# The order table of a fused linear-attention and MLP kernel is replaced by another one

## The chip, the cores and the metric

The kernel runs on one core of a Trainium2 chip. The metric is the device time of one execution in microseconds (us). The engines are PE (TensorE), DVE (VectorE), ACT (ScalarE), POOL (GpSimd) and SP (SyncE), which here only issues DMAs. Each works through its own list of instructions in order; semaphores make one engine wait for another.

## The reference

Two stages: a linear attention with a decaying state, and a two-layer MLP on its output.

```python
for t in range(S):                                   # B, H, S, D = 4, 8, 768, 48
    kt, vt, rt = (k[:, :, t], v[:, :, t], r[:, :, t])
    cur = np.einsum('bhd,bhe->bhde', u[None] * kt, vt)
    y[:, :, t] = np.einsum('bhd,bhde->bhe', rt, state + cur)
    state = w[None, :, :, None] * state + np.einsum('bhd,bhe->bhde', kt, vt)
x = y.transpose(0, 2, 1, 3).reshape(3072, 384)
h = x @ w_in                                         # 384 x 2048
sp = np.maximum(h, 0.0) + np.log1p(np.exp(-np.abs(h)))
out = (h * erf(sp)) @ w_out                          # 2048 x 384
```

## The kernel before

The sequence is cut into chunks of 128 steps, four batches each: 24 chunks, numbered 0 to 23, four of which fill one block of 512 tokens for the MLP. There are six blocks (0 to 5). The MLP takes 16 pieces of 128 of its 2048 hidden columns per block, so 96 MLP steps, numbered 0 to 95. Block 0 does its first eight pieces (steps 0 to 7), then block 1 its first eight (8 to 15), then the two finish (16 to 31), and the other blocks follow whole. MLP step 8 is therefore the first that needs block 1, that is, chunks 4 to 7.

All work is written as short words in a table, `ORDER`. A loop reads the table and issues the instructions of each word; the order of the words is the order of the instructions on every engine, since each engine keeps the order in which it was given work. Numbers in a word are those of the chunk or the MLP step. A `+` at a word's end puts it on POOL, a `*` on ACT, nothing on DVE (or on the one engine that can do it). The words, with the lines of the profile:

- `L4a`, `L4b`: load the two halves of chunk 4 (L66, L69), 512 and 608 KB. `U0` loads `ub` (L76). `F12` loads a piece of a weight as 64-bit words (L102; first digit 0 for `w_in`, 1 for `w_out`), 768 KB, into one of two `raw` buffers. `C12a` to `C12f` turn that piece into two fp32r parts (L118 to L130; `a` and `e` are on ACT, the rest on DVE, `f` may be on POOL) in one `wt` buffer, so pieces follow each other.
- `K`, `R`, `N` (L187, L191, L195) scale a chunk; `Qa`, `Qb`, `Qc` (L212, L215, L219) make the diagonal's sums `q`; `M70`, `M71` (L230 on ACT, L232 elsewhere) write them into `am`; `A7` (L249, PE) makes the chunk's scores; `P70`, `P71` (L255, DVE) merge the scores into `am`; `Y7` (L272, PE) is the chunk's output; `X7a`, `X7b` (L312 ACT, L315 DVE) write it into the block's `x`. `D7` (L291, PE) is the state's update, `S7a` to `S7d` (L303 to L309) add it to `sbd`.
- An MLP step n: `f` (L338, PE, nine matmuls `x`,`wih`/`wil` to `h`), `a b z c d e g` (the activation, ACT except `z` and `g`, L345 to L370), `h` (L376, ACT) and `l` (L381, DVE or POOL) split it into `gh` and `gl`, and `p` (L397, PE, nine matmuls into `acc`).
- `W8` issues eight matmuls on zeros (L87, `dummy`), which only keep PE at work.

Chunks live in three buffers of one pool (chunk 3 in another): a load waits until an earlier chunk's last reader is done. `h` has three PSUM buffers; `A`, `D` and, from chunk 4 on, `Y` share two more. SP's list is in order too: a load behind a waiting one waits with it.

Of the kernel before, what the change touches and what calls it, by code (L numbers as in the profile page):

```python
# [615 lines left out]
S0b S0a L3a C00a P01 Q1b+ Q2c W7 A2 L3b N2 M21* C00b Y0 N1 M20* C00c D2 L4a K3+ S2b X0a S2a X0b L4b P20 R3 W7 D1 C00d
Q3a C00e F01 S1b K4+ Q1c P21 M11* C00f+ S1a W11 Y2 M10* P11 Q3b+ X2a P10 C10a Q4a W4 Y1 C10b Q3c N3+ A3 X1a L5a X2b
M30* X1b R4+ D3 L5b S3a M31* P30 C10c L6a P31 R5+ L6b S3b W10 A4 K5 Q4b Y3 C10d X3a R6 F11 C10e X3b N4+ W4 f0 Q4c Q6a+
M41* Q5a+ M40* P41 f1 Q5b+ a0 P40 b0 N5+ Q5c z0 A5 a1 M50* C10f K6 b1 P50 C01a z1 W7 Y4 M51* C01b C01c c0 c1 C01d X4a
d1 X4b F02 C01e Q6b P51 e1 C01f+ d0 g1 W11 A6 e0 Q6c f2 M60* g0 N6 C11a P60 h0 f3 C11b h1 l0 a2 C11c M61* C11d Y5 b2  # L620
l1 F03 C11e z2 a3 p0 C11f X5a b3 X5b C02a P61 p1 c2 C02b d2 C02c e2 z3 D6 g2 c3 Y6 C02d h2 d3 l2 F12 C02e S6a p2 S6b
e3 C02f X6a g3 S6d+ C03a X6b f4 h3 C03b C03c C03d D5 a4 f5 S5a b4 F13 S5b C03e S5d z4 S5c c4 C03f D4 a5 f6 d4 S4a L7a
l3 C12a S4c S6c L7b e4 C12b b5 g4 p3 a6 C12c L8a h4 b6 R7 C12d f7 Q7a C12e F05 l4 C12f p4 R8 L9a C13a z5 Q7b+ z6 c5
# [1 line left out]
g6 L10b S7d+ Q8c h6 Q9a+ S7a M80* C13c f9 a8 C13d M81* R9 F14 C13e l5 A8 b8 l6+ z7 p5 P81 a9 C13f+ c7 P80 b9 z8 d7 A9
c8 Q10a+ e7 p6 d8 Q9b+ g7 C14a Q10b+ Q9c e8 f10 h7 M90+ g8 M91* Q10c l7+ P90 h8 P91 f11 a10 l8+ z9 b10 c9 N10 C14b p7
d9 N9 a11 C14c O70a b11 O70b C14d O71a Y9 e9 O71b S7c N8 C14e g9 D8 C14f h9 f12 O72a l9 C05a O72b z10 C05b c10 p8 z11
a12 C05c d10 c11 C05d e10 p9 d11 g10 F04 C05e S4d R10 h10 C05f f13 e11 F15 b12 g11 l10 h11 z12 f14 l11+ a13 C04a K10
c12 C04b b13 p10 C04c a14 d12 C04d b14 e12 p11 z13 F06 C04e g12 c13 C04f h12 f15 d13 l12 C15a z14 e13 C15b c14 p12 g13
a15 C15c d14 h13 C15d e14 f16 b15 l13+ F16 g14 C15e h14 z15 C15f+ p13 a16 c15 b16 l14 C06a f17 z16 d15 C06b c16 C06c  # L630
e15 d16 p14 C06d a17 e16 g15 F07 C06e g16 f18 h15 C06f h16 l15 b17 C16a l16+ z17 p15 a18 O150a C16b c17 O150b C16c
O151a f19 d17 O151b C16d b18 e17 F17 z18 C16e g17 O152a C16f f20 h17 O152b c18 l17 C07a p16 d18 C07b a19 C07c e18 b19
g18 p17 a20 z19 h18 C07d b20 c19 l18+ f21 C07e d19 C07f e19 z20 C17a p18 g19 a21 C17b h19 C17c b21 f22 c20 l19 d20
C17d e20 z21 C17e p19 g20 c21 C17f a22 d21 f23 X9a e21 X9b h20 g21 b22 l20 h21 Y8 z22 a23 l21+ c22 b23 p20 S8a L11a
M100+ S8b d22 z23 X8a M101+ e22 L11b X8b c23 g22 p21 d23 S8c S8d h22 R11 e23 K11 A10 O230a g23 l22+ O232a h23 f24 P101
Q11a+ P100 l23 f25 Q11b+ a24 b24 Q11c N11+ z24 A11 M110 a25 c24 M111 p22 b25 P111 d24 z25 e24 P110 c25 p23 g24 d25
O230b h24 e25 O230c l24+ Y11 g25 O232b h25 O232c l25+ D11 X11a f26 O231a S11a S11b S11c+ X11b S11d D9 a26 Y10 S9a L12a
b26 S9c O231b z26 O231c f27 X10a S9b L12b c26 S9d X10b d26 R12 e26 f28 a27 g26 b27 K12 z27 Q12a+ f29 c27 a28 Q12b d27
Q12c N12+ b28 A12 e27 M120+ a29 g27 M121* p24 P120 b29 P121 p25 h26 l26 z28 Y12 c28 h27 d28 l27+ D12 X12a e28 f30 X12b
g28 S12b S12a S12d+ z29 f31 a30 S12c c29 b30 d29 D10 a31 p26 S10b L13a e29 S10d b31 g29 S10a L13b S10c p27 h28 L14a  # L640
l28 R13+ z30 L14b p28 c30 K13+ h29 d30 L15a e30 l29 A13 R14 L15b z31 K14+ p29 g30 c31 h30 Q13a d31 Q13b f32 l30 O311a
e31 N13 O312a Q13c R15+ g31 M130* p30 M131+ a32 P130 h31 K15 b32 f33 P131 l31+ z32 Q15a c32 p31 Q15b a33 d32 Q15c N15+
b33 O311b e32 z33 Y13 O311c O312b c33 g32 O312c d33 D13 Q14a X13a f34 e33 S13a L16a S13b S13c+ h32 X13b S13d+ g33
O310a l32 h33 L16b f35 Q14b a34 l33+ Q14c b34 M140* z34 K16+ O310b f36 a35 O310c M150* R16+ p32 c34 Q16a a36 Q16b d34
N14 b35 M141 e34 A15 z35 N16+ b36 g34 c35 p33 M151+ P150 h34 d35 P151 e35 l34 f37 g35 z36 h35 Q16c c36 l35+ f38 a37
d36 b37 e36 z37 p34 a38 g36 c37 b38 d37 f39 h36 e37 l36+ g37 p35 a39 z38 b39 c38 d38 f40 h37 e38 l37 g38 Y15 a40 z39
b40 c39 D15 X15a d39 f41 S15b S15d e39 X15b g39 S15a f42 S15c a41 b41 A14 p36 P140 P141 p37 h38 l38 z40 Y14 a42 c40
b42 d40 D14 M161 X14a p38 L17a S14b e40 X14b S14d+ h39 S14a g40 S14c+ L18a l39 f43 h40 z41 L18b l40+ c41 d41 L17b z42
A16 a43 R18+ e41 p39 P161 c42 K18+ b43 g41 d42 Q18a+ e42 p40 h41 g42 Q17a+ l41 f44 h42 Q17b+ z43 c43 l42 d43 Q18b f45
a44 Q17c N18+ e43 b44 g43 z44 p41 a45 M171 c44 N17 b45 K17 d44 p42 R17 h43 M160 e44 M170 g44 f46 l43 h44 z45 l44+ Q18c  # L650
c45 f47 P160 a46 d45 b46 e45 z46 Y16 a47 g45 c46 b47 d46 p43 M180 X16a M181+ e46 X16b g46 p44 h45 l45 z47 p45 c47 h46
d47 l46+ e47 A17 g47 h47 p46 P171 l47+ P170 Y17 D17 X17a f48 X17b S17b S17a S17d+ S17c+ f49 a48 b48 z48 f50 c48 a49
d48 b49 e48 A18 z49 a50 g48 c49 p47 P181 h48 b50 l48 d49 P180 O470a f51 z50 O472a O470b e49 O472b c50 g49 d50 Y18 a51
h49 e50 l49+ D16 X18a g50 f52 L19a b51 S16b O471a S16d S16a L20a z51 S16c+ X18b p48 c51 L20b a52 d51 R19 b52 K19+
O471b p49 e51 h50 L19b g51 K20+ A19 h51 R20+ f53 Q20a l50 l51+ z52 p50 c52 Q20b+ a53 d52 Q19a+ Q20c b53 p51 e52 z53
N20+ g52 c53 Q19b+ h52 f54 d53 l52+ Q19c e53 g53 M191+ f55 h53 M201+ a54 P191 b54 l53+ z54 f56 a55 N19+ c54 b55 M190+
d54 z55 p52 a56 P190 e54 c55 g54 b56 p53 d55 h54 e55 l54+ M200* g55 f57 z56 h55 c56 l55 d56 f58 a57 e56 b57 g56 p54
z57 a58 b58 c57 d57 p55 h56 e57 l56 z58 f59 g57 c58 h57 d58 l57+ e58 A20 a59 g58 p56 b59 P200 P201 z59 p57 h58 c59
l58+ d59 e59 p58 g59 h59 l59+ f60 p59 a60 b60 z60 f61 c60 d60 e60 g60 f62 a61 h60 b61 l60 z61 p60 a62 c61 b62 d61 z62
f63 e61 c62 g61 d62 h61 D19 e62 l61+ Y19 a63 g62 b63 h62 p61 S19a X19a S19c S19b l62+ X19b z63 S19d p62 c63 d63 e63  # L660
g63 f64 h63 l63 p63 a64 b64 O630a z64 O631a O630b f65 c64 O631b d64 e64 f66 g64 a65 O632a b65 O632b h64 z65 f67 a66
l64+ c65 b66 d65 z66 p64 a67 c66 e65 d66 g65 D18 b67 Y20 S18a L21a h65 S18c e66 S18b l65+ g66 L21b f68 X20a S18d+ z67
h66 X20b l66+ c67 L22a d67 p65 a68 K21+ L22b e67 b68 R21 L23a f69 z68 Q21a+ g67 c68 L23b K22+ h67 d68 f70 Q22a+ a69
e68 l67+ b69 g68 A21 a70 Q22b+ z69 b70 p66 R23+ Q22c c69 d69 Q21b e69 N21 p67 h68 R22 M220* Q23a Q21c Q23b+ g69 f71
M210+ h69 N23+ P210 f72 a71 N22 l68 b71 l69 z70 p68 M211 a72 c70 M221+ P211 b72 z71 p69 d70 Q23c c71 K23 e70 d71 g70
Y21 e71 h70 g71 l70 h71 f73 X21a M231+ z72 M230* X21b l71 c72 f74 a73 d72 b73 e72 z73 A22 a74 g72 c73 p70 P221 b74 d73
P220 e73 g73 p71 h72 l72+ f75 z74 h73 c74 l73+ d74 f76 e74 a75 g74 b75 z75 f77 a76 c75 b76 d75 A23 a77 e75 p72 b77 g75
P231 P230 f78 h74 l74+ z76 Y23 c76 a78 d76 p73 b78 X23a e76 X23b Z0 g76 p74 h75 l75+ f79 z77 h76 c77 l76+ d77 p75 e77
z78 a79 g77 c78 b79 d78 Y22 h77 e78 l77 g78 p76 X22a X22b z79 c79 f80 h78 d79 l78 e79 g79 p77 a80 b80 z80 p78 c80 h79
d80 l79+ e80 f81 g80 h80 l80 p79 a81 b81 O790a z81 O791a O790b f82 c81 O791b d81 e81 f83 g81 a82 O792a b82 O792b h81  # L670
z82 f84 a83 l81+ c82 b83 d82 z83 p80 a84 e82 b84 g82 c83 p81 h82 d83 l82 e83 z84 p82 g83 c84 h83 d84 l83+ e84 f85 g84
h84 l84 f86 a85 b85 z85 p83 c85 a86 d85 b86 p84 e85 z86 g85 c86 h85 d86 f87 l85+ e86 g86 h86 p85 a87 l86 b87 z87 p86
c87 d87 e87 f88 g87 h87 l87+ f89 a88 b88 z88 f90 c88 a89 d88 b89 p87 e88 z89 a90 g88 c89 h88 f91 b90 l88 d89 z90 e89
c90 g89 p88 a91 d90 b91 h89 f92 e90 l89+ g90 h90 z91 p89 a92 l90+ c91 b92 d91 z92 f93 e91 c92 g91 d92 h91 f94 a93 l91+
# [67 lines left out]
```

## Time and profile before

| | us |
|---|---|
| median of three runs (528.63 to 529.61) | 529.5 |
| the profiled execution | 532.55 |
| its span, first to last instruction | 530.7 |
| PE busy | 512.3 |
| ACT busy | 397.1 |
| DVE busy | 348.6 |
| POOL busy | 170.5 |

The span is the part of the profiled execution that the trace covers; 1.85 us lie around it. Busy times are sums over the whole span; the stages differ, so the views by stage matter more. "Idle before" a group is the time its engine stood still ahead of it, with the engine that ended the wait.

### The profile page before, as it was taken

The page shows a single profiled execution, that of the slowest core. Times are in us where ns is not written, and L with a number is a line of the kernel's source. Part 1 is how long each engine was busy: PE and PEld are TensorE (multiplying, and loading weights), DVE is VectorE, ACT ScalarE, POOL GpSimd, SP SyncE. Part 2 cuts the span into 40 slices and gives each one's busy share as a digit, 9 for nine tenths or more (in the row PEclk, how much of TensorE's full clock was granted, in tenths as well). Part 3 has the DMA queues.
Part 4 walks back from the last instruction along what each step waited for, and adds up shares of the span by engine and source line. Part 5 has one row for each costly group of instructions (what it writes and reads, how often), then busy time and mean ns, then how long its engine had stood idle before and what let it go on. Part 6 is the DMA issues. An engine that isn't in the chain of part 4 may idle for free.

```text
span 530.7 us, 10435 instructions
## 1 busy us (share of the span) xinstructions
PE 512.3 (97%) x4151; PEld 395.7 (75%) x4159; DVE 348.6 (66%) x609; ACT 397.1 (75%) x757; POOL 170.5 (32%) x152
## 2 busy tenths in 40 slices
...
PEclk9999996999999999999999999999999999999999
...
GB/s 304 315 238 67 94 234 230 91 172 76 159 72 127 101 156 211 23 147 1 42 134 1 1 137 98 2 0 2 41 278 3 1 2 1 41 20 1 1 1 65
DMA packets 13863, 48.91 MB, mean 92 GB/s; under 512 B 1648, under 2 KB 1776, under 8 KB 13808
## 3 DMA queue, kind: packets, MB, share of 16 engines
...
q8 instruction: 35, 0.57, 0.5%
...
## 4 chain that ended last, share of the span: by engine, by line
PE 82%; DVE 9%; ACT 6%; DMA 1%; issue 1%; SPq 0%; DVEq 0%; ACTq 0%
PE acc L397 36%; PE h L338 35%; PE y L272 6%; PE A L249 3%; ACT am L230 2%; DMA att<-in_att_dram 1%; PE ds L291 1%; DVE am L255 1%; DVE att L191 1%; DVE s L354 1%; DVE wt L122 1%; DVE wt L125 1%; ACT s L345 1%; ACT s L362 1%; DVE q L219 1%
## 5 line engine op out<-in xcount | busy, mean ns | idle before, releaser
L338 PE MATMUL h<-x,wih 128*128 128x512 f32 x576 | 184.7, 402 | 2.3 <-DVE x L315 1.1
L381 POOL TENSOR_TENSOR gl<-s,gh 128x512 fp32r<-128x512 f32 x48 | 64.5, 1344 | 225.4 <-ACT gh L376 207.9
L338 PEld LDWEIGHTS h<-x,wih 128*128 128x128 f32 x576 | 107.9, 190 | 30.4 <-DVE s L370 2.0
L397 PE MATMUL acc<-gh,woh 128*128 128x512 f32 x288 | 116.3, 404 | 0.0
L338 PE MATMUL h<-x,wil 128*128 128x512 f32 x288 | 114.6, 398 | 0.0
L397 PE MATMUL acc<-gh,wol 128*128 128x512 f32 x288 | 113.8, 395 | 0.3 <-DVE wol L130 0.3
L397 PE MATMUL acc<-gl,woh 128*128 128x512 f32 x288 | 113.8, 395 | 0.3 <-DVE gl L381 0.2
L370 DVE SCALAR_TENSOR_TENSOR s<-s,h 128x512 f32<-128x512 f32 x96 | 65.6, 684 | 61.6 <-ACT s L366 61.2
L354 DVE SCALAR_TENSOR_TENSOR s<-s,h 128x512 f32<-128x512 f32 x96 | 65.6, 684 | 49.9 <-ACT s L349 39.7
L376 ACT CAST gh<-s 128x512 fp32r<-128x512 f32 x96 | 58.9, 616 | 36.0 <-PE acc L397 17.5
L358 ACT ACTIVATE s<-s 128x512 f32<-128x512 f32 x96 | 60.1, 627 | 29.1 <-DVE s L354 28.8
L345 ACT ACTIVATE s<-h 128x512 f32<-128x512 f32 x96 | 56.7, 591 | 26.9 <-PE h L338 23.0
L397 PEld LDWEIGHTS acc<-gh,woh 128*128 128x128 f32 x288 | 54.2, 188 | 15.9 <-issue 2.6
L338 PEld LDWEIGHTS h<-x,wil 128*128 128x128 f32 x288 | 54.7, 190 | 13.2 <-DVE wil L130 0.4
L397 PEld LDWEIGHTS acc<-gh,wol 128*128 128x128 f32 x288 | 54.2, 188 | 13.3 <-DVE wol L130 0.7
L397 PEld LDWEIGHTS acc<-gl,woh 128*128 128x128 f32 x288 | 54.2, 188 | 12.9 <-DVE gl L381 1.0
L366 ACT ACTIVATE s<-s 128x512 f32<-128x512 f32 x96 | 60.3, 628 | 1.1
L362 ACT ACTIVATE s<-s 128x512 f32<-128x512 f32 x96 | 60.1, 626 | 0.9
L349 ACT ACTIVATE s<-s 128x512 f32<-128x512 f32 x96 | 60.1, 626 | 0.8
L255 DVE COPY_PREDICATED am<-mask,A 64x256 f32<-64x256 uint32 x96 | 39.5, 443 | 13.2 <-ACT am L230 5.2
L381 DVE TENSOR_TENSOR gl<-s,gh 128x512 fp32r<-128x512 f32 x48 | 36.1, 753 | 17.3 <-ACT gh L376 17.1
L230 ACT ACTIVATE am<-ident,q 128x128 f32<-128x128 f32 x100 | 31.3, 390 | 8.8 <-DVE q L219 8.7
...
## 6 DMA issues: line engine op xcount, KB each, us to landing
...
att<-in_att_dram SPq DMA_DIRECT2D x24, 512.0 KB, 4.0
raw<-in_win_dram SPq DMA_DIRECT2D x8, 768.0 KB, 4.4
raw<-in_wout_dram SPq DMA_DIRECT2D x8, 768.0 KB, 4.2
...
```

Of the source, the lines that this page charges most:

```text
L255: nc.vector.copy_predicated(out=am[r, :, c], data=ap[r, :, c], mask=m[r, hh:hh + 1, c].to_broadcast([r.stop - r.start, NPAIR, H]))
L338: nc.tensor.matmul(out=h, lhsT=w[:, f, q, :], rhs=x[:, xi, q, :], start=k == 0, stop=k == 8)
L345: nc.scalar.activation(out=s1, in_=e["h"], func=AF.Tanh, bias=FB0, scale=FA0)
L349: nc.scalar.activation(out=s1, in_=s1, func=AF.Tanh, bias=FB1, scale=FA1)
L354: nc.vector.scalar_tensor_tensor(out=e["s"], in0=e["s1"], scalar=FG, in1=e["h"], op0=ALU.mult, op1=ALU.add)
L358: nc.scalar.activation(out=s, in_=s, func=AF.Tanh, bias=FB2, scale=FA2)
L362: nc.scalar.activation(out=s, in_=s, func=AF.Square, bias=FB3, scale=FA3)
L366: nc.scalar.activation(out=s, in_=s, func=AF.Square, bias=FB4, scale=FA4)
L370: nc.vector.scalar_tensor_tensor(out=s, in0=s, scalar=FC, in1=ff[n]["h"], op0=ALU.subtract, op1=ALU.mult, reverse0=True)
L376: nc.scalar.copy(out=e["gh"], in_=e["s"])
L381: eng.tensor_tensor(out=e["gl"], in0=e["s"], in1=e["gh"].bitcast(F32), op=ALU.subtract)
L397: nc.tensor.matmul(out=acc[e], lhsT=w[:, f, es], rhs=g, start=first and i == 0, stop=last and i == 2)
```

## The change

Only the table changes: 1717 words become 1719. The computation's words are the same in both; what differs is their order, which engine some of them are put on (`K3`, for instance, moves from POOL to DVE), and the dummy words: 73 matmuls in ten words become 70 in twelve. The start of the table and the rows that lead to `f8`, cut from the diff:

```diff
-L0a L1a U0 L0b R0 L2a T0 K0 Q0a+ L2b A0 K1 L1b R1 K2 W4 A1 R2 F00 Q0b Q2a+ Q0c M00* N0 F10 Q2b+ W8 D0 M01* P00 Q1a+
+U0 L0a L0b L1a R0 T0 L2a K0 Q0a W1 A0 Q0b L3a Q0c N0+ M01* L2b K1+ W4 D0 S0b M00* P01 R1+ S0a F00 P00 W7 A1 R3 K3 Y0
...
-L8b K7+ Q7c a7 S4b d5 N7+ M71* L9b A7 M70+ e5 P71 b7 K8+ P70 c6 D7 g5 d6 Y7 Q8a e6 K9 h5 C13b X7a L10a S7b Q8b+ X7b f8
+L7b c6 z7 S4c+ d6 p5 C13b c7 C13c L8a e6 d7 K7 L8b R7 e7 Q7a A7 g7 Q7b+ L9a g6 Q7c h6 L9b C13d M70* N7 M71* F05 l6+
+P70 C13e P71 K9+ h7 Y7 l7+ R9+ D7 X7a L10a X7b f8 C13f L10b Q9a C05a S7a S7b S7c+ p6 a8 S7d C05b b8 C05c p7 C05d O70a
```

The first place is on DVE, around the sum `q7` of chunk 7 (L219), the last chunk of block 1. Before:

```order
L191 TENSOR_TENSOR att8_1040<-att8_1040,wr_110 112x512
L354 SCALAR_TENSOR_TENSOR s2_5_1078<-s1_5_1001,h5_970 128x512
L354 SCALAR_TENSOR_TENSOR s2_6_1081<-s1_6_1037,h6_1003 128x512
L219 TENSOR_REDUCE q7_1086<-att7_1015 128x8
L305 TENSOR_TENSOR sbd_143<-sbd_143,ds4_992 48x4x48
L255 COPY_PREDICATED am7_1_1093<-mask_94,A7_1_1100 64x4x64
```

and after:

```order
L187 TENSOR_TENSOR att7_1076<-att7_1076,wk_111 112x512
L191 TENSOR_TENSOR att7_1076<-att7_1076,wr_110 112x512
L212 TENSOR_TENSOR att7_1076<-att7_1076,ub_85 128x384
L370 SCALAR_TENSOR_TENSOR s2_7_1084<-s2_7_1084,h7_1030 128x512
L370 SCALAR_TENSOR_TENSOR s2_6_1061<-s2_6_1061,h6_993 128x512
L219 TENSOR_REDUCE q7_1132<-att7_1076 128x8
L125 SCALAR_TENSOR_TENSOR wt13_1074<-raw13_955,wt13_1074 128x768
```

The scaling of chunk 7 by `wk` is now on DVE and stands just ahead of the sum, and so do the steps `g7` and `g6` of the MLP; ahead of `q7` DVE has 157 instructions, where it had 152.

The second place is on PE, the end of the work ahead of chunk 7's scores. Before:

```order
L397 MATMUL acc0_1_841<-gl_4_1061,woh_91 128x512
L397 MATMUL acc0_1_841<-gh_4_1042,wol_92 128x512
L397 MATMUL acc0_2_842<-gh_4_1042,woh_91 128x512
L397 MATMUL acc0_2_842<-gl_4_1061,woh_91 128x512
L397 MATMUL acc0_2_842<-gh_4_1042,wol_92 128x512
L249 MATMUL A7_0_1099<-att7_1015 64x128
```

and after:

```order
L397 MATMUL acc0_1_790<-gl_5_1063,woh_91 128x512
L397 MATMUL acc0_1_790<-gh_5_1047,wol_92 128x512
L397 MATMUL acc0_2_791<-gh_5_1047,woh_91 128x512
L397 MATMUL acc0_2_791<-gl_5_1063,woh_91 128x512
L397 MATMUL acc0_2_791<-gh_5_1047,wol_92 128x512
L249 MATMUL A7_0_1109<-att7_1076 64x128
```

The word `p5` has moved ahead of `A7`; otherwise PE has the same useful words ahead of `f8` in both tables. Behind `f8` the runs of attention words (`A`, `Y`, `D`) that interrupt the MLP's matmuls number 37, where they were 34.

The third place is on POOL, the work that leads to the step `Qb` of chunk 7 (L215). Before:

```order
L130 TENSOR_TENSOR wil_90<-wt01_656,wih_89 128x768
L309 TENSOR_TENSOR sbd_143<-sbd_143,wp_109 48x4x48
L215 TENSOR_TENSOR att7_1015<-att7_1015 128x384
L187 TENSOR_TENSOR att7_1015<-att7_1015,wk_111 112x512
L195 TENSOR_TENSOR att7_1015<-att7_1015,wkn_142 128x384
L232 TENSOR_TENSOR am7_0_1117<-ident_93,q7_1086 128x512
```

and after:

```order
L130 TENSOR_TENSOR wil_90<-wt01_604,wih_89 128x768
L195 TENSOR_TENSOR att6_591<-att6_591,wkn_142 128x384
L130 TENSOR_TENSOR wol_92<-wt11_807,woh_91 128x768
L309 TENSOR_TENSOR sbd_143<-sbd_143,wp_109 48x4x48
L381 TENSOR_TENSOR gl_3_989<-s2_3_887,gh_3_973 128x512
L309 TENSOR_TENSOR sbd_143<-sbd_143,wp_109 48x4x48 x2
L381 TENSOR_TENSOR gl_5_1063<-s2_5_1007,gh_5_1047 128x512
L309 TENSOR_TENSOR sbd_143<-sbd_143,wp_109 48x4x48 x2
L215 TENSOR_TENSOR att7_1076<-att7_1076 128x384
```

Between the weight piece `wt01` and chunk 7 POOL had one instruction and now has nine; the scaling of chunk 7 and the writing of `am7` (both `M70` and `M71` are now on ACT) have left it. On SP the loads of chunk 7 now stand behind the load of the weight piece `raw14`, which stood behind chunks 7 to 10 before.

More of the change, by code (lines that the diff above doesn't have):

```diff
@@ L614 @@
 ORDER = """
-L0a L1a U0 L0b R0 L2a T0 K0 Q0a+ L2b A0 K1 L1b R1 K2 W4 A1 R2 F00 Q0b Q2a+ Q0c M00* N0 F10 Q2b+ W8 D0 M01* P00 Q1a+
[L616 to L623, printed above, removed]
-L8b K7+ Q7c a7 S4b d5 N7+ M71* L9b A7 M70+ e5 P71 b7 K8+ P70 c6 D7 g5 d6 Y7 Q8a e6 K9 h5 C13b X7a L10a S7b Q8b+ X7b f8
@@ L625 @@
[L625 to L674, printed above, removed]
@@ L675 @@
-e92 b93 g92 p90 z93 a94 b94 c93 d93 p91 h92 e93 l92+ g93 f95 h93 z94 l93 c94 d94 p92 a95 e94 b95 g94 z95 p93x h94 p93y
-c95 l94 d95 p93z e95 p94x g95 p94y h95 p94z l95 p95x p95y O950a p95z O950b O951a O951b O952a O952b
+U0 L0a L0b L1a R0 T0 L2a K0 Q0a W1 A0 Q0b L3a Q0c N0+ M01* L2b K1+ W4 D0 S0b M00* P01 R1+ S0a F00 P00 W7 A1 R3 K3 Y0
+F10 R2 K2 Q2a W2 A2 X0a L1b Q2b C00a Q2c N2+ X0b M21* C00b W4 D2 L3b C00c M20* S2b C00d Q1a C00e F01 Q1b C00f+ Q1c P20
+M11* L4a P21 M10* Q3a+ P11 W20 Y2 L4b Q3b+ S2a C10a P10 X2a C10b W2 Y1 R4 X2b K4+ A3 X1a Q3c X1b M30* N3 N1 W2 D3 M31*
@@ new lines @@
+Q4a D1 S3a Q4b+ L5a S1a P30 P31 L5b C10c W7 A4 C10d Y3 R5 C10e F02 S1b K5+ X3a Q4c X3b M41* W4 f0 S3b L6a Q5a C10f
+M40* L6b P41 Q5b+ C01a f1 P40 N5+ a0 Q5c b0 M50+ M51* z0 A5 R6+ a1 P50 c0 C01b b1 W3 Y4 C01c d0 e0 z1 X4a C01d c1 d1
+X4b F11 K6 C01e g0 e1 C01f+ P51 h0 g1 W14 A6 l0 C02a f2 N4 h1 C02b C02c l1 f3 a2 C02d b2 z2 C02e F03 Q6a p0 c2 C02f a3
+d2 Q6b C11a Q6c N6+ p1 M61* C11b C11c M60* f4 C11d b3 P60 C11e F12 P61 e2 C11f+ Y5 a4 g2 b4 z3 h2 f5 X5a l2 C03a X5b
+c3 C03b d3 C03c Y6 a5 e3 C03d b5 D6 g3 F13 X6a p2 C03e S6b S6a S6d+ z4 h3 S6c c4 C03f d4 D5 X6b l3+ C12a f6 S5a S5b e4
@@ new lines @@
+S5c+ z5 S5d+ g4 c5 p3 C12b a6 d5 C12c h4 C12d e5 f7 b6 g5 F14 C12e l4 h5 C12f D4 a7 z6 l5+ p4 C13a L7a S4b S4a b7 S4d+
+L7b c6 z7 S4c+ d6 p5 C13b c7 C13c L8a e6 d7 K7 L8b R7 e7 Q7a A7 g7 Q7b+ L9a g6 Q7c h6 L9b C13d M70* N7 M71* F05 l6+
+P70 C13e P71 K9+ h7 Y7 l7+ R9+ D7 X7a L10a X7b f8 C13f L10b Q9a C05a S7a S7b S7c+ p6 a8 S7d C05b b8 C05c p7 C05d O70a
+z8 C05e O70b K10 f9 c8 Q8a O72a Q8b d8 K8 O72b e8 Q10a f10 R8 a9 O71a g8 Q10b+ b9 O71b Q8c h8 N8+ Q10c A8 z9 a10 l8+
+b10 f11 c9 M81+ z10 d9 e9 C05f+ P81 c10 p8 a11 g9 d10 M80 h9 b11 N10 f12 P80 e10 l9+ C14a g10 z11 h10 A9 a12 C14b c11
@@ new lines @@
+C14c p9 b12 d11 C14d e11 Q9b F04 C14e g11 f13 N9+ Q9c h11 l10+ M91* F06 f14 C14f+ z12 M90* P91 c12 P90 a13 p10 l11
+C04a R10 b13 C04b a14 z13 p11 d12 C04c c13 b14 C04d d13 e12 D9 F15 Y9 C04e g12 e13 C04f h12 f15 g13 C06a l12+ S9a S9b
+h13 S9d+ z14 f16 l13 a15 C06b c14 b15 C06c d14 D8 C06d a16 p12 e14 z15 F07 b16 g14 C06e S9c c15 C06f f17 h14 d15 l14
+C15a z16 p13 e15 C15b a17 g15 c16 C15c b17 f18 d16 C15d h15 e16 F16 l15 C15e z17 p14 a18 C15f c17 b18 g16 C07a p15 d17
+C07b O150a C07c O151a O150b e17 f19 C07d O151b h16 g17 C07e F17 l16 h17 f20 C07f a19 O152a l17 C16a O152b z18 p16 b19
@@ new lines @@
+C16b c18 C16c a20 d18 z19 p17 b20 C16d e18 C16e g18 c19 C16f f21 h18 d19 l18 C17a z20 p18 e19 C17b c20 g19 a21 C17c
+d20 f22 b21 C17d e20 C17e g20 h19 C17f f23 h20 l19 a22 X9a z21 b22 p19 X9b a23 l20 c21 b23 z22 d21 p20 c22 e21 d22 g21
+e22 Y8 h21 g22 l21 h22 z23 f24 l22+ M100* L11a S8b S8a c23 S8c+ L12a S8d+ X8a p21 d23 X8b a24 M101 e23 K11 b24 g23 p22
+O231a z24 R12+ h23 L11b c24 K12+ d24 A10 O232a e24 L12b g24 f25 l23 h24 R11 P100 l24+ f26 a25 P101 b25 Q11a+ z25 Q11b+
+f27 c25 a26 Q12a+ Q11c d25 b26 N11 M110* A11 z26 Q12b+ p23 Q12c N12+ c26 P110 a27 d26 O231b e25 e26 Y10 O231c g25 b27
```

39 lines of the change are left out of this document (added).

## The prediction

> **What bounds the kernel now.** I read the page first, then the windows, and then the timelines of the stretch that stands out.
>
> ```profile
> span 530.7 us, 10435 instructions
> PE 512.3 (97%) x4151; PEld 395.7 (75%) x4159; DVE 348.6 (66%) x609; ACT 397.1 (75%) x757; POOL 170.5 (32%) x152
> PEclk9999996999999999999999999999999999999999
> ```
>
> PE is busy 97% of the span, and its clock is full in every fortieth but the seventh (80 to 93 us).
>
> ```profile
> 60.00:80.00 20.00, 19.69 (x172) 14.95 (x171) 19.72 (x34) 14.83 (x25) 3.20 (x2) 1.00 0.56 188
> 80.00:100.00 20.00, 16.77 (x175) 12.40 (x177) 15.31 (x28) 13.67 (x32) 13.45 (x12) 0.74 0.56 207
> 100.00:120.00 20.00, 20.00 (x176) 16.12 (x174) 17.93 (x30) 18.75 (x35) 5.33 (x5) 1.00 0.36 119
> 480.00:520.00 40.00, 40.00 (x174) 32.36 (x173) 16.08 (x24) 33.31 (x60) 7.79 (x6) 1.00 0.00 1
> ```
>
> The columns are PE, weight loads, DVE, ACT, POOL, granted clock. Up to 80 us DVE has no air (19.72 of 20); from 100 us on PE is full, to the end. So the order can matter in one place only: how soon PE gets enough work to stay full. That is decided at MLP step 8, which waits for chunk 7.
>
> ```profile
> 80.81 0.39 PE L397 MATMUL acc<-gh,wol 128*128 128x512 f32 x1
> 81.87 0.43 PE L249 MATMUL A<-att 48*64 48x128 f32 x2 [0.67 <-POOL att L187]
> 82.87 1.05 PE L249 MATMUL A<-att 48*64 48x128 f32 x30 [0.57 <-DVE sbd L305]
> 85.31 0.88 PE L291 MATMUL ds<-att 128*48 128x48 f32 x16 [1.38 <-DVE am L255]
> 86.12 1.51 PE L272 MATMUL y<-att,sbd 112*32 112x128 f32 x24
> 87.40 1.94 PE L272 MATMUL y<-am,att 128*32 128x128 f32 x32
> 89.94 1.39 PE L338 MATMUL h<-x,wih 128*128 128x512 f32 x2 [0.60 <-ACT x L312]
> 86.00:88.00 2.00, 2.00 (x41) 1.78 (x41) 1.97 (x5) 1.47 (x3) 1.17 (x1) 0.50 0.00 0
> ```
>
> PE ends `p4` at 81.2, gets `A7` late, waits for `am`, runs `D7` and `Y7` at half clock (0.50), and starts `f8` at 89.94. From there to the end of the span are 530.7 - 89.94 = 440.8 us.
>
> **The change part by part.** *PE's own list.* Ahead of `f8` the new list holds one word more, `p5`; the rest of its useful words is the same. So what follows `f8` is shorter by one `p`:
>
> ```profile
> 59.91 2.09 PE acc L397 x9
> 64.16 2.29 PE acc L397 x9
> ```
>
> 2.1 us less. The second row is such a word behind an attention word: 0.2 us more. Behind `f8` there are 37 runs of attention words instead of 34, so 3 x 0.2 = 0.6 us more. The change ends where the old kernel does if `f8` starts 2.1 - 0.6 = 1.5 us later, at 91.4.
>
> *DVE up to `q7`.* The sum `q7` stands behind 157 instructions of DVE instead of 152: five more `Qa`/`Qb`, three `g`, a `z`, two steps of a weight piece, against fewer `R`, `N`, `S` and a `Cf`.
>
> ```profile
> 50.90:77.20 26.30, 26.30 (x267) 20.44 (x259) 25.72 (x45) 22.28 (x42) 1.91 (x2) 1.00 0.49 173
> 81.80 0.54 DVE L219 TENSOR_REDUCE q<-att 128x8 f32<-128x384 f32 x1
> 11.03 0.69 DVE L187 TENSOR_TENSOR att<-att,wk 112x512 f32<-112x512 f32 x1 [1.27 <-DMA att<-in_att_dram]
> 14.72 0.77 DVE L255 COPY_PREDICATED am<-mask,A 64x256 f32<-64x256 uint32 x2 [0.66 <-ACT am L230]
> 40.28 0.92 DVE L255 COPY_PREDICATED am<-mask,A 64x256 f32<-64x256 uint32 x2 [1.35 <-ACT am L230]
> ```
>
> Where DVE is full it passes 45 instructions in 26.3 us, 0.58 each, so five are 2.9 us. Its long waits ahead of `q7` are the three last rows, 3.3 us: that much of the new work could fall into waits and cost nothing; this is the lower end. I take none of it off: the first wait is filled by chunk 0's `Qa`, `Qb`, `Qc`, which now stand there, but `R5` stands on DVE behind a load that waits for chunk 1's `D1`, and `D1` has moved behind `Y1` and `A3`, so a new wait stands against it.
>
> *POOL beside DVE.*
>
> ```profile
> 75.76 0.69 DVE L191 TENSOR_TENSOR att<-att,wr 112x512 f32<-112x512 f32 x1
> 79.17 1.51 DVE L191 TENSOR_TENSOR att<-att,wr 112x512 f32<-112x512 f32 x1
> 78.01 2.12 POOL L215 TENSOR_TENSOR att<-att 128x384 f32<-128x384 f32 x1 [11.76 <-DVE att L212]
> ```
>
> The same operation took 0.69 alone and 1.51 while POOL was at work. POOL had one instruction between the weight piece `wt01` and chunk 7, with 11.76 us of idle time behind it; now it has nine there. Between none and three such meetings cost 0 to 3 x 0.82 = 2.5 us; I take one, 0.8, since most of DVE's steps there read PSUM or wait for nobody. `q7`, over at 82.34, is then over at 82.34 + 2.9 + 0.8 = 86.0. [...]
>
> *From `q7` to `f8`.* Before, ACT wrote `am7_1` and POOL `am7_0` side by side; now ACT writes both.
>
> ```profile
> 24.72 2.45 ACT L230 ACTIVATE am<-ident,q 128x128 f32<-128x128 f32 x8 [0.60 <-DVE q L219]
> 27.20 0.77 DVE L255 COPY_PREDICATED am<-mask,A 64x256 f32<-64x256 uint32 x2 [0.25 <-ACT am L230]
> 89.41 0.48 ACT L312 CAST x<-y 128x384 fp32r<-128x384 f32 x1 [1.91 <-PE y L272]
> ```
>
> Both take 2.45 us: 88.5. `P70` hides beside the second, `P71` is 0.8: 89.3. `Y7`: 3.2 at half clock, as before (86.12 to 89.34): 92.5. Its way into `x` takes 0.6 (89.34 to 89.94): `f8` at 93.1, or 3.2 later. PE meanwhile idles from `A7`'s end, some 84, to 89.3, longer than before, so the half clock stays in the sum. The sum: 3.2 - 1.5 = 1.7 us later.
>
> *Loads.* Chunk 7's load stands on SP behind that of `raw14`, which waits for the last reader of `raw12`, nine rows of DVE ahead of `K7`: 9 x 0.58 = 5.2 us.
>
> ```profile
> att<-in_att_dram SPq DMA_DIRECT2D x24, 512.0 KB, 4.0
> raw<-in_wout_dram SPq DMA_DIRECT2D x8, 768.0 KB, 4.2
> ```
>
> It lands 4.0 us after its issue, more if the piece ahead delays it: 0 to 1 us of wait for `K7`, taken as 0, with DVE's own queue as the cover; without it 1 us.
>
> *Dummies, and everything behind `f8`.* Three fewer dummies are under a microsecond, all in waits of the start: 0. The block of twenty ahead of `Y2` would delay `Y2` only if its `am` came earlier than the block's end. Six `l` moved from POOL to DVE, eight state steps the other way and five `am` to ACT cost nothing, since ACT is at 33.31 and DVE at 16.08 of 40 us late; with that cover gone, each is its own length.
>
> The profiled execution took 532.55: span 530.7 and 1.85 around it; the median of the runs, 529.5, is 3.05 lower. I add the difference to the median: 529.5 + 1.7 = 531.2.
>
> **The rivals.** *Faster: the new start of DVE keeps what it gains.* If all three waits of the start are filled (3.3 us) and no meeting with POOL costs anything (0.8), `f8` starts at 93.1 - 4.1 = 89.0: 1.7 - 4.1 = -2.4, 527.1; with the waits alone, 528. For it: the first stages have DVE idle, and the new order puts work there that needs one chunk only. Against it: DVE was full from 40 to 80 us, and the extra five stand before `q7` anyway. It decides once 2.8 us are saved (1.7, and the 1.1 that tell from no change).
>
> *No change.* About half of those waits is filled: 1.7 - 1.7 = 0.0, 529.5. This is also the case in which the change does not do what it says, the early loads opening waits of the same size.
>
> *More slowly: POOL.* Three meetings instead of one: 1.7 + 1.7 = 3.4, 532.9.
>
> *The clock.* Half clock cost 0.88 + 3.2 - 2.2 = 1.9 us on `D7` and `Y7` and 2.3 on `f8` and `f9`:
>
> ```profile
> 89.94 6.68 PE h L338 x18
> 51.57 4.38 PE h L338 x18
> ```
>
> If the timed runs of the old kernel escape it (their median lies 3.05 under the profiled run) and the new kernel, with its longer gap, does not, the difference grows by 4.2: 535.4. [...]
>
> **How the numbers follow.** Chances: the forecast, 530.6 to 532.4, 0.30; no change 0.27; faster 0.29; POOL 0.10; the clock 0.04. A difference under 0.2% (1.1 us) is about what a measurement of this kernel cannot tell from none. Slower: 0.30 + 0.10 + 0.04 = 0.44. The range runs from the case with all waits filled, 527.0, to a little over the POOL case, 534.0; the likeliest case alone is 530.6 to 532.4.
>
> **What would show it.** Right: DVE's reduce of `q7` ends near 86; one run of eight `am` instructions on ACT behind it; PE idle for about five us between `A7` and `Y7`; granted clock 0.5 around 90; `f8` near 93 with PE full behind it. Wrong: `f8` at 91 or earlier; DVE rows near 60 to 80 us with idle time in them (then the five extra cost nothing); a clock that stays full between 80 and 100; a wait of several us on PE anywhere behind 100.

## The result, and the profile after

| us | before | after |
|---|---|---|
| median of the timed runs (4 each) | 529.56 | 535.38 (535.08 to 536.94) |
| the profiled execution | 532.55 | 535.46 |
| its span | 530.7 | 533.8 |
| PE busy | 512.3 | 512.4 |
| sum `q7` over | 82.3 | 83.4 |
| `Y7` starts | 86.1 | 86.7 |
| `f8` starts | 89.9 | 90.6 |

The new order is slower: the ratio is 1.011, with a 95% interval of 1.0086 to 1.0134, or 5.8 us. The direction was the forecast one; the time lies above the range, and most of the loss has another place and another size. The profiled execution of the old kernel, 532.55, was one with a long half clock, above all its timed runs then; the spans of the two profiles, 3.1 us apart, therefore understate the change. Two runs that took more than twice as long as all others, one of the old kernel (1131.73 us) and one of experiment 2 (1738.06 us), are left out of the ratios below.

The page after: the span and the engines' sums are as they were, but the row of the granted clock has a second dent, in the thirty-second of its forty slices (413.7 to 427.0 us).

```profile
span 533.8 us, 10442 instructions
PE 512.4 (96%) x4156; PEld 396.1 (74%) x4156; DVE 349.4 (65%) x607; ACT 403.9 (76%) x777; POOL 158.5 (30%) x149
PEclk9999997999999999999999999999999799999999
```

The windows place both dents. Their columns are PE, weight loads, DVE, ACT, POOL, granted clock, DMA share and GB/s; the first row is the old kernel's, the others are the new one's:

```profile
400.00:440.00 40.00, 40.00 (x350) 31.76 (x350) 25.20 (x42) 29.94 (x59) 11.48 (x11) 1.00 0.00 1
80.00:100.00 20.00, 14.76 (x145) 11.96 (x144) 16.50 (x29) 11.41 (x24) 7.29 (x7) 0.83 0.64 246
400.00:440.00 40.00, 35.59 (x294) 27.90 (x292) 26.57 (x35) 27.48 (x56) 17.08 (x15) 0.91 0.00 1
413.00:419.00 6.00, 5.23 (x12) 4.13 (x13) 3.21 (x6) 4.13 (x8) 3.76 (x3) 0.50 0.00 0
```

From 80 to 100 us PE is idle for 5.2 us, from 400 to 440 us for 4.4, where the old kernel had PE at work for 40.00 of 40. That second stretch is late in the kernel, where I had put the cost at nothing.

**The way to `f8`**, in the timelines of DVE, ACT and PE of the new kernel:

```profile
79.62 0.69 DVE L187 TENSOR_TENSOR att<-att,wk 112x512 f32<-112x512 f32 x1
80.97 1.09 PE L249 MATMUL A<-att 48*64 48x128 f32 x32 [0.64 <-DVE att L191]
82.87 0.55 DVE L219 TENSOR_REDUCE q<-att 128x8 f32<-128x384 f32 x1
83.52 2.44 ACT L230 ACTIVATE am<-ident,q 128x128 f32<-128x128 f32 x8
86.66 1.51 PE L272 MATMUL y<-att,sbd 112*32 112x128 f32 x24 [4.60 <-DVE am L255]
89.80 0.88 PE L291 MATMUL ds<-att 128*48 128x48 f32 x16
90.62 1.10 PE L338 MATMUL h<-x,wih 128*128 128x512 f32 x2
```

`q7` is over at 83.42, 1.1 us later than before and not 3.7. `D7` now stands in PE's wait for `x`, between `Y7` and `f8`, which were 0.6 us apart in the old kernel with PE idle.

**The stall at 409 to 414 us.** PE ends `A21` and waits 4.4 us for the `h` buffer of `f73` (step 73), that is, for `g70`, the last reader of step 70's `h`:

```profile
408.27 1.09 PE L249 MATMUL A<-att 48*64 48x128 f32 x32
413.77 1.22 PE L338 MATMUL h<-x,wih 128*128 128x512 f32 x2 [4.41 <-DVE s L370]
```

Followed back, in the timelines of DVE and ACT (in the new order `R21`, the sum `Q21c`, `M210`, the activations `b70` and `c70` to `e70`, and `g70`):

```profile
399.40 7.93 DVE L191 TENSOR_TENSOR att<-att,wr 112x512 f32<-112x512 f32 x1
407.25 0.54 DVE L219 TENSOR_REDUCE q<-att 128x8 f32<-128x384 f32 x1
407.83 1.28 ACT L230 ACTIVATE am<-ident,q 128x128 f32<-128x128 f32 x4 [5.14 <-DVE q L219]
409.66 0.69 DVE L354 SCALAR_TENSOR_TENSOR s<-s,h 128x512 f32<-128x512 f32 x1 [1.87 <-ACT s L349]
413.02 0.69 DVE L370 SCALAR_TENSOR_TENSOR s<-s,h 128x512 f32<-128x512 f32 x1 [1.47 <-ACT s L366]
```

The first row is where the loss begins. `R21` is an operation that takes 0.69 us when alone (the prediction has that row) and here stands for 7.93. What POOL did in that time:

```profile
397.75 1.28 POOL L187 TENSOR_TENSOR att<-att,wk 112x512 f32<-112x512 f32 x1
399.00 0.85 POOL L309 TENSOR_TENSOR sbd<-sbd,wp 48x192 f32<-48x192 f32 x1
399.81 1.00 POOL L215 TENSOR_TENSOR att<-att 128x384 f32<-128x384 f32 x1
400.79 1.28 POOL L381 TENSOR_TENSOR gl<-s,gh 128x512 fp32r<-128x512 f32 x1
402.03 1.28 POOL L187 TENSOR_TENSOR att<-att,wk 112x512 f32<-112x512 f32 x1
403.28 2.52 POOL L191 TENSOR_TENSOR att<-att,wr 112x512 f32<-112x512 f32 x2
405.77 1.01 POOL L212 TENSOR_TENSOR att<-att,ub 128x384 f32<-128x384 f32 x1
406.86 1.35 POOL L215 TENSOR_TENSOR att<-att 128x384 f32<-128x384 f32 x1
```

Each row begins before the one ahead of it has ended, up to 406.78 (405.77 + 1.01). There is the first gap, 0.08 us, and there `R21` gets in: it is over at 407.33, and the POOL instruction behind the gap takes 1.35 us, where the same form takes 1.00 at 399.81. The gap is the one place in the row at which POOL waits for its own result (`Q23b` reads what `Q23a` wrote). So `R21` stood behind seven instructions of POOL: the one at work when it started (399.00 to 399.85), and six more.

`R21` is on DVE in the old order too, and it met POOL there as well. Its row and the POOL rows beside it, before:

```profile
392.81 1.61 DVE L191 TENSOR_TENSOR att<-att,wr 112x512 f32<-112x512 f32 x1
392.57 1.30 POOL L381 TENSOR_TENSOR gl<-s,gh 128x512 fp32r<-128x512 f32 x1 [0.29 <-POOL sbd L309]
393.83 1.74 POOL L187 TENSOR_TENSOR att<-att,wk 112x512 f32<-112x512 f32 x1
```

There it got in at the end of the first POOL instruction, although the next one began without a gap, and lost 0.9 us. What the change did was to put five words of this place on POOL that had been on DVE: `S18c`, `Q21b`, `l69`, `R22` and `Q23a`. They are five of the seven words in the row behind which `R21` then stood.

### The profile page after: what moved, and what is told of

It is laid out like the page before. It is cut to its first block, busy times and chain, and to the rows that moved or that the text cites. A ratio compares the mean times of both kernels' runs of the same rounds, so it can differ in the third digit from the quotient of the medians.

```text
span 533.8 us, 10442 instructions
## 1 busy us (share of the span) xinstructions
PE 512.4 (96%) x4156; PEld 396.1 (74%) x4156; DVE 349.4 (65%) x607; ACT 403.9 (76%) x777; POOL 158.5 (30%) x149
## 4 chain that ended last, share of the span: by engine, by line
PE 80%; DVE 6%; ACT 5%; DMA 4%; issue 2%; POOL 1%; SPq 0%; DVEq 0%; POOLq 0%; ACTq 0%
PE h L338 36%; PE acc L397 34%; PE y L272 6%; DMA att<-in_att_dram 4%; PE A L249 3%; PE ds L291 1%; DVE am L255 1%; ACT s L358 1%; DVE s L370 1%; DVE wt L125 1%; ACT am L230 1%; ACT s L362 1%; ACT s L349 1%; ACT s L366 1%; DVE att L191 1%
## 5 line engine op out<-in xcount | busy, mean ns | idle before, releaser
L381 POOL TENSOR_TENSOR gl<-s,gh 128x512 fp32r<-128x512 f32 x42 | 56.4, 1344 | 212.0 <-ACT gh L376 210.8
L370 DVE SCALAR_TENSOR_TENSOR s<-s,h 128x512 f32<-128x512 f32 x96 | 65.4, 684 | 63.1 <-ACT s L366 62.7
L354 DVE SCALAR_TENSOR_TENSOR s<-s,h 128x512 f32<-128x512 f32 x96 | 65.8, 685 | 47.3 <-POOL gl L381 24.2
L381 DVE TENSOR_TENSOR gl<-s,gh 128x512 fp32r<-128x512 f32 x54 | 38.3, 709 | 26.1 <-ACT gh L376 25.6
L230 ACT ACTIVATE am<-ident,q 128x128 f32<-128x128 f32 x120 | 37.2, 390 | 8.9 <-DVE q L219 8.9
```

Source lines behind the costliest of these rows:

```text
L354: nc.vector.scalar_tensor_tensor(out=e["s"], in0=e["s1"], scalar=FG, in1=e["h"], op0=ALU.mult, op1=ALU.add)
L370: nc.vector.scalar_tensor_tensor(out=s, in0=s, scalar=FC, in1=ff[n]["h"], op0=ALU.subtract, op1=ALU.mult, reverse0=True)
L381: eng.tensor_tensor(out=e["gl"], in0=e["s"], in1=e["gh"].bitcast(F32), op=ALU.subtract)
```

## The experiments

All are compared with runs of the old kernel on the same chip; a ratio below 1 is faster than the old kernel. The new kernel's own ratio is 1.011. Where the expectations say `f75`, it is `f73` that waits.

**1. `R21` on POOL.**

```diff
-R21
+R21+
```

> The new order with one word changed: R21 (the scaling of chunk 21 by wr) is put on POOL instead of DVE. Theory A (POOL holds DVE): in the new kernel this step stood 7.93 us on DVE instead of 0.69, behind a row of POOL instructions without a gap; the steps z and g of the MLP behind it came late, PE stood 4.4 us at f75 and its clock then fell to half for 6.8 us (about 2.3 us more). Without it the kernel gains 4.4 + 2.3 = 6.7 us: 535.4 to 528.7, PE full and its clock full between 400 and 420 us. Rival B (ACT's list: M210 stands on ACT ahead of the activations of steps 70 and 71 and is what blocks): M210 still waits for the sum of chunk 21, which comes later still, since POOL's row is one longer; the stall stays: 535 to 537. Rival C (the loss is made at the start of the kernel): no change, 535.4.

Measured: 529.41 us, ratio 0.9988 (0.9975 to 1.0002). The waits of PE behind 60 us are now:

```profile
PE y L272 <- DVE am L255: 4.6, 1, 4.6
PE A L249 <- DVE att L191: 0.6, 1, 0.6
PE h L338 <- DVE s L370: 0.4, 1, 0.4
PE acc L397 <- DVE gl L381: 0.2, 1, 0.2
```

The 4.4 us are down to 0.4 and the second dent of the clock is gone. One letter of 1719 words carries the whole loss; what is left of the change can't be told from none. Rival B expected no gain, since the sum of chunk 21 would come later still; it came earlier (402.50 instead of 407.25). Rival C, a loss at the start, falls too.

**2. The gap earlier.** The same POOL work; only the place at which POOL waits for itself moves forward.

```diff
-K22+ b70 p69 R23+ a71 z70 b71 R22+ c70 z71 f72 d70 Q23a+ c71 e70 Q23b+
+Q23a+ Q23b+ K22+ b70 p69 R23+ a71 z70 b71 R22+ c70 z71 f72 d70 c71 e70
```

> The new order with Q23a and Q23b moved ahead of K22 on POOL: the same POOL work, but the one place at which POOL waits for its own result (Q23b behind Q23a) comes after two instructions of the row instead of five. Theory A, with DVE let in only at such a gap: R21 on DVE ends about 3.7 us earlier (some 4.2 us long instead of 7.93), PE's wait at f75 falls from 4.4 to about 0.7 and the clock stays full: 535.4 - 3.7 - 2.3 = 529.4. If it is the sum of POOL's work and not the gap that counts: R21 as long as before, 535.4. Rival B or C: 535.4.

Measured: 529.64 us, ratio 0.9987 (0.9966 to 1.0009). DVE and POOL:

```profile
399.43 4.18 DVE L191 TENSOR_TENSOR att<-att,wr 112x512 f32<-112x512 f32 x1
402.06 1.00 POOL L212 TENSOR_TENSOR att<-att,ub 128x384 f32<-128x384 f32 x1
403.14 1.35 POOL L215 TENSOR_TENSOR att<-att 128x384 f32<-128x384 f32 x1
```

`R21` is 4.18 us long and runs in the gap at 403.06. `R21` is let in where the gap stands, not when POOL's work is done.

**3. The row longer.**

```diff
-Q23a+
+K23+ Q23a+
...
-K23+
```

> The new order with K23 (1.28 us on POOL) moved ahead of Q23a, into the row that holds R21. Theory A: R21 stands 7.9 + 1.3 = 9.2 us, PE's wait at f75 is 4.4 + 1.3 = 5.7 us: 535.4 + 1.3 = 536.7. Rival B, C: 535.4.

Measured: 536.59 us, ratio 1.012 (1.0095 to 1.0145).

```profile
400.15 9.18 DVE L191 TENSOR_TENSOR att<-att,wr 112x512 f32<-112x512 f32 x1
415.77 1.22 PE L338 MATMUL h<-x,wih 128*128 128x512 f32 x2 [5.25 <-DVE s L370]
```

Three lengths of the row, three lengths of `R21`: 4.18, 7.93 and 9.18 us, and the end of the kernel follows.

**4. `M210` off ACT.**

```diff
-M210*
+M210
```

> The new order with M210 (the first write of am for chunk 21) on DVE instead of ACT, so that ACT does not stand behind the sum of chunk 21. Theory A: R21 still takes 7.9 us, and z70 on DVE stands behind it; only ACT's four instructions and its own delay are saved: about 1.2 us, 534.2. Rival B (ACT's list is what blocks): the whole 6.7 us come back, 528.7. Rival C: 535.4.

Measured: 533.83 us, ratio 1.0069 (1.0045 to 1.0092). `R21` still took 7.95 us, and PE waited 3.21 us instead of 4.41. So ACT's list adds 1.2 us to the stall and does not make it.

**5. `S18c` on DVE, and 6. `R21` later.**

```diff
-S18c+
+S18c
```

> The new order with the state step S18c on DVE instead of POOL, the first instruction of the row in which R21 waited. What is open is why R21 lost six turns to POOL while elsewhere DVE got in after one instruction of POOL. Theory E (it depends on how the row starts, POOL's first instruction having been held by DVE's Q21a just before): R21 gets in after one POOL instruction, 1.3 to 2 us long, PE's wait goes: 529.4. Theory F (any row of POOL without a gap keeps DVE out): R21 still stands until the gap ahead of Q23b, 7 us: 535.4.

Measured: 529.09 us, ratio 0.9965 (0.9945 to 0.9985). The stall is gone, but the run does not choose between E and F: the step on DVE shifted `R21`, which now started just before POOL's next instruction and met nothing.

```profile
401.05 0.68 DVE L191 TENSOR_TENSOR att<-att,wr 112x512 f32<-112x512 f32 x1
401.20 1.40 POOL L215 TENSOR_TENSOR att<-att 128x384 f32<-128x384 f32 x1 [0.78 <-DVE att L212]
```

Here POOL is the one that waits (1.40 instead of 1.00). POOL had stood idle for 0.78 us, and `R21` began 0.15 us ahead of it: 0.68 us, where it took 7.93 when POOL was at work as it came.

```diff
-R21 L23b Q21b+ l69+ Q21c f71 a70 M210* K22+ b70 p69 R23+ a71 z70 b71 R22+ c70
+L23b Q21b+ l69+ Q21c f71 a70 M210* K22+ b70 p69 R23+ a71 z70 b71 R22+ R21 c70
```

> The new order with R21 left on DVE but moved behind z70 and z71, so that the sum of chunk 21 and the activations do not stand behind it. It then meets the same row of POOL nearer its end. Theory A: whatever R21 loses there, the MLP's steps are ahead of it; PE's wait at f75 goes: 529 to 530. If a late R21 holds A21 and Y21 up instead: 531 to 533.

(`R21` stands behind `z70`, ahead of `z71`.) Measured: 530.22 us, ratio 0.9993 (0.9975 to 1.0011).

```profile
405.05 2.35 DVE L191 TENSOR_TENSOR att<-att,wr 112x512 f32<-112x512 f32 x1
```

It lost the turn at 405.83 to `Q23a` and ran, again, in the gap ahead of `Q23b`; but the activations of step 70 were ahead of it, and PE's longest wait there was 0.6 us.

**7. and 8. The place of `D7`,** in the old kernel and, mirrored, in the new one with `R21` on POOL.

```diff
-P70 c6 D7 g5 d6 Y7 Q8a e6 K9 h5 C13b X7a L10a S7b Q8b+ X7b f8
+P70 c6 g5 d6 Y7 D7 Q8a e6 K9 h5 C13b X7a L10a Q8b+ X7b S7b f8
```

> The kernel before with one thing of the new order: D7 behind Y7 instead of ahead of it (and S7b behind X7b). Theory A (why the new order loses less behind f8 although its f8 starts later): with D7 in PE's wait for x, PE has work without a gap up to f8 and the half clock ends one window of 3.4 us sooner (it lasted 10.2 us before and 6.8 us in the new order), worth about 1.9 us, and Y7 starts about 0.4 us sooner: 529.5 - 2.0 to 2.3 = 527.3. Rival D (the place of D7 does not matter, the half clock ends by itself at a fixed time): -0.4 at most, 529.1 to 529.5.

Measured: 530.59 us, ratio 1.0004 (0.9988 to 1.0021): no gain, rival D by the ratio. The granted clock of its 12 runs is 0.991 to 0.997, so the longest half clock (0.987 to 0.989 in the old kernel) is gone; but only one run is at 0.997, a value that 23 of the old kernel's 92 runs reach or pass.

```diff
-Y7 l7+ R9+ D7 X7a
+D7 Y7 l7+ R9+ X7a
```

> The mirror: the new order with R21 on POOL (529.4 measured), and D7 ahead of Y7 as in the kernel before. Theory A: the wait for x is empty again, the half clock lasts a window longer, and Y7 starts up to 0.9 us later: 529.4 + 1.5 to 2.5 = 531.4. Rival D: +0 to 0.9, 529.4 to 530.3.

Measured: 532.25 us, ratio 1.003 (1.0011 to 1.0049), against 0.9988 with `D7` behind `Y7`: 2.2 us, as theory A had it.

```profile
90.10 1.93 PE L272 MATMUL y<-am,att 128*32 128x128 f32 x32
92.64 1.39 PE L338 MATMUL h<-x,wih 128*128 128x512 f32 x2 [0.61 <-ACT x L312]
94.00:96.00 2.00, 2.00 (x7) 1.52 (x6) 1.90 (x6) 0.91 (x1) 0.50 (x1) 0.50 1.01 397
```

The wait for `x` is empty again and the clock is still at 0.50 in the window of 94 to 96 us. Of its 12 runs 6 have a granted clock of 0.989 or less, and of experiment 1's none (0.990 to 0.996). So the place of `D7` is worth something where the clock has fallen. In the old kernel it does not always fall (see the last section); that this is why experiment 7 gained nothing is likely, but not shown.

**9. The old kernel with `R8` behind `q7`.**

```diff
-R8 L9a C13a
+L9a C13a
...
-Y7 Q8a
+Y7 R8 Q8a
```

> The kernel before with R8 (which stood 1.51 us on DVE instead of 0.69, since POOL was at work) moved from ahead of the sum q7 to behind P70. Theory (what the prediction had the wrong way round: it was the old order that met POOL ahead of q7, three times for 1.8 us, and the new one not at all): q7 ends up to 1.3 us sooner, f8 0.7 to 1.3 us sooner: 528.5. Rival: q7 waits for Qb on POOL or for ACT instead and f8 stays: 529.5.

Measured: 528.72 us, ratio 0.997 (0.9954 to 0.9987). `R8` took 1.51 us ahead of `q7` in the old kernel, where POOL's `Q7b` was at work until 80.13, and takes 0.68 here at its new place (84.29).

```profile
79.67 0.55 DVE L219 TENSOR_REDUCE q<-att 128x8 f32<-128x384 f32 x1
83.89 0.86 PE L272 MATMUL y<-att,sbd 112*32 112x128 f32 x24
PEclk9999999999999999999999999999999999999999
```

`q7` is over at 80.2 instead of 82.3, 2.1 us sooner where at most 1.3 were forecast; `Y7` starts at 83.9, and in the profiled execution the clock did not fall. One word moved makes the old kernel 0.3% faster. The run does not price the meeting alone: the move took the word's own 0.69 us from ahead of `q7` too, and 7 of the 12 runs have a granted clock of 0.997 or more, against 23 of the old kernel's 92.

**10. `M70` on POOL.**

```diff
-Q7c h6 L9b C13d M70* N7 M71* F05 l6+ P70 C13e P71 K9+
+Q7c N7 h6 L9b M70+ M71* C13d F05 P71 P70 l6+ C13e K9+
```

> The new order with R21 on POOL, and in the way to f8: M70 on POOL beside M71 on ACT, N7 right behind the sum q7, P71 and P70 ahead of l6. Theory: am7 is whole about 0.9 us sooner, Y7 and f8 too: 529.4 - 0.9 = 528.5. Rival: POOL's M70 and DVE's N7 lock each other out, or l6 and l7 come later and p6 and p7 stall: 529.4 or a little more.

Measured: 529.89 us, ratio 1.0 (0.9984 to 1.0017), no gain, as its rival has it. `C13d` took 1.80 us beside `M70` on POOL instead of 0.95, and the merges of the scores (`P71`, `P70`) started at 85.64, where they start at 85.75 in the new kernel; `Y7` started at 87.35, against 86.85 in experiment 1.

**11. `p5` into the gap.**

```diff
-p5 C13b c7 C13c
+C13b c7 C13c
...
-Y7 l7+ R9+
+p5 Y7 l7+ R9+
```

> The new order with R21 on POOL, and p5 moved from ahead of A7 to between A7 and Y7: the same PE work ahead of f8, but the idle time of 0.6 + 4.6 us is cut into two pieces of some 2.7 us. Theory (the half clock comes from the long gap): if neither piece makes the clock fall, Y7, D7 and f8 run at full clock: 529.4 - 1.8 = 527.6. Rival (idle time as such makes it fall, in pieces as well): 529.4 to 530.5.

Measured: 528.14 us, ratio 0.9964 (0.9946 to 0.9983). The gain is near the forecast one, but not in its way:

```profile
80.00:82.00 2.00, 0.96 (x24) 0.96 (x26) 1.77 (x4) 0.78 (x2) 0.10 (x1) 0.62 1.02 420
84.00:86.00 2.00, 2.00 (x6) 1.61 (x5) 2.00 (x3) 2.00 (x8) 2.00 (x2) 0.50 1.08 397
88.00:90.00 2.00, 1.88 (x53) 1.26 (x41) 0.50 (x2) 0.48 (x1) 2.00 (x2) 1.00 0.13 53
```

The clock fell all the same, only earlier, and `p5` ran at half clock in a time in which PE had to wait for `am` anyway; `Y7`, `D7` and `f8` then ran at full clock.

**12. A faster version.** On top of experiment 1: the loads of chunk 7 ahead of that of `raw14`, `C13c` behind `q7` and `C13d` further back (the expectation names `C13b` too, but by the table it still stands just ahead of `Q7c`), `N7` right behind `q7`, `l6` on DVE.

```diff
-F14 C12e l4
+L7a L7b F14 C12e l4
...
-C13a L7a S4b S4a b7 S4d+ L7b c6 z7 S4c+ d6 p5 C13b c7 C13c
+C13a S4b S4a b7 S4d+ c6 z7 S4c+ d6 p5 c7
...
-K7 L8b R7 e7 Q7a A7 g7 Q7b+ L9a g6 Q7c h6 L9b C13d M70* N7 M71* F05 l6+ P70 C13e P71 K9+ h7 Y7 l7+
+K7 L8b R7 e7 Q7a Q7b+ A7 L9a g6 C13b Q7c N7 h6 L9b g7 C13c M71* M70* F05 h7 P71 P70 C13d C13e l6 l7+ K9+ Y7
```

> A version meant to be faster than both. The new order with R21 on POOL; the loads of chunk 7 ahead of that of raw14; the steps C13b, C13c, C13d of a weight piece moved from ahead of the sum q7 to behind it; N7 right behind q7; l6 on DVE behind P70. By the rows of the new kernel q7 should end near 81.6 instead of 83.4, Y7 start near 84.5 instead of 86.7 and f8 near 88.5 instead of 90.6: 529.4 - 2.1 = 527.3, and about 1 less if the clock then stays up in some runs. Rival: C13 comes late for p6 or q7 waits for POOL's Qb, and nothing is gained: 529.4.

Measured: 528.53 us, ratio 0.9957 (0.9942 to 0.9973), faster than both kernels. Its profiled execution, at 530.03 the longest of its runs, does not show the forecast step, though: `q7` is over at 83.6 and `f8` starts at 91.1, no sooner than in the new kernel. `C13b`, still ahead of the sum, took 1.04 us there beside POOL's `Q7b`, where it takes 0.55 alone. What gains in this version is open.

## Why the prediction was wrong

*What bounds the kernel.* "The order can matter in one place only" is the sentence that failed. It was read from the old kernel's windows, in which PE is full behind 100 us. That shows what the old order did there, not what another order can do: in the new one a single operation of DVE, `R21`, was held long enough (7.93 us) to use up the cover of three `h` buffers.

*PE's own list.* `p5` and the longer list ahead of `f8` came out as worked out. In experiment 1, `f8` starts at 90.81 and the span ends 437.2 us later, against 440.8: 3.6 less. The step had 1.5. Of the other 2.1, half clock behind `f8` is 1.8: it lasted until 94.6 in the old profile and until 91.9 in this one, so 4.7 and 1.1 us of it are behind `f8`, by my estimate of half speed worth 2.35 and 0.55 (in experiment 11 the matmuls of `p5`, at a clock of 0.50, started 0.43 us apart, and those of the next `p`, at 1.00, 0.23). Some 0.2 are shorter waits.

*DVE up to `q7`.* Here the sum was 3.7 us and the trace says 1.1. The POOL term had the wrong sign: I charged the new order with one meeting, 0.8 us. The old order had four ahead of `q7`, by these rows of its DVE (the fourth is the 1.51 in the prediction):

```profile
13.29 0.77 DVE L195 TENSOR_TENSOR att<-att,wkn 128x384 f32<-128x384 f32 x1
28.37 1.32 DVE L120 TENSOR_SCALAR wt<-wt 128x768 int32<-128x768 int32 x1
36.39 1.49 DVE L191 TENSOR_TENSOR att<-att,wr 112x512 f32<-112x512 f32 x1
```

Against 0.55, 0.55 and 0.69, what these three forms take alone in the same trace, and with the 0.8 of the fourth, that is 0.2 + 0.8 + 0.8 + 0.8 = 2.6 us. The new order has three short ones, at 32.23, 42.56 and 56.22 us, of 0.1, 0.1 and 0.3. So the change took away 2.1 us there (the expectation of experiment 9 has three meetings for 1.8, and none in the new order). DVE's idle time up to `q7` shrank by 0.7 as well (8.0 to 7.3), a part of the waits of which I took none off. What is left says that DVE's own work ahead of `q7` grew by 1.1 + 2.1 + 0.7 = 3.9 us, not by 2.9: five instructions at the mean pace of 0.58 were too cheap. The prediction's reason for charging one meeting only has the old trace behind it where it names PSUM: `z` and `g`, which read `h` there, took 0.684 us on average over 96 each (L354, L370). Experiment 9 shows that `R8` stood on the path; it does not tell the meeting's share from the word's own length.

*From `q7` to `f8`.* Worked out as 7.1 us, measured 7.2; both `M7` on ACT, the half clock and PE's wait of about five microseconds (4.60) are as described. That `D7` moved behind `Y7` I had not used; in the profile of experiment 1 the half clock is over at 91.9 us, in that of experiment 8, with `D7` ahead of `Y7`, the clock is still at 0.50 from 94 to 96 us.

*The rival "more slowly: POOL"* had the right mechanism with the wrong place and a wrong price: three meetings at 0.82 near `q7`. It was one, of 7.24 us (7.93 less 0.69), at 399 us. The price came from rows in which DVE waits for one instruction of POOL; I had no row in which it waits for several, and put no bound on that.

*"Everything behind `f8`" at zero* is the step that failed and the term that was mis-sized: the words moved between DVE and POOL were costed by their own lengths and their engines' mean load (DVE 16.08 of 40). What such a word does to an operation of the other engine was not asked there, and the prediction's list has the `l`, the state steps and the `am`, but not the `Q` and `R` words, three of the five that made the row (`Q21b`, `R22`, `Q23a`). Its measured price: by the ratios of the new kernel and experiment 1, 1.22%, or 6.5 us; by the rows, 4.0 us of wait (4.4 less the 0.4 that stay) and up to 2.7 of half clock (413.8 to 419.1 us at half speed).

*The clock rival* gave 535.4, the time that was measured, but by coincidence and not for its reason. It had one true half: the old kernel's runs mostly escape the long half clock of its profile (21 of 92 have a granted clock of 0.987 to 0.989, the profile 0.988), while in the new kernel and in experiment 1 the clock fell in every run (0.996 at most). Without `R21`'s stall that costs nothing that can be told from none (0.9988).

The account of the change: the start and PE's list give about -0.6 us (experiment 1, with an interval that reaches to 0.1), the held `R21` gives +6.5, together the 5.8 measured, but for rounding. What stays open is why `R21` got in at once in the old order and lost every turn in the new one. Of the signs named ahead, two for "wrong" came: `f8` ahead of 91, and a wait of several microseconds on PE behind 100.
